# Four attention output chunks inside the first two FFN units, operand sums on VectorE, and LN2's mean from the residual add

## The chip, the cores and the metric

The kernel runs on one core of one Trainium2 chip. The metric is device time in microseconds (us) for one execution, the median over runs. The engines are named as in the profile: PE (TensorE, matrix products; PEld is its weight load), DVE (VectorE), ACT (ScalarE), POOL (GpSimd) and SP, which only issues DMA transfers here.

## What is computed

The input is one sequence of 2048 tokens with 1024 features, in bf16. Two blocks follow each other: linear attention with 32 heads, and a gated FFN with 3584 hidden features. A conditioning vector gives each block a shift, a scale and a gate.

```python
mod = silu(c) @ w_mod                    # six vectors: sa, ca, ga, sb, cb, gb
h = layernorm(x) * (1 + ca) + sa
q, k, v = heads(h @ wqkv)                # 32 heads of 32
pq, pk = phi(q), phi(k)                  # phi(t) = where(t > 0, t + 1, exp(t)) + 1e-6
o = (pq @ (pk^T v)) / (pq . sum(pk) + 1e-6)
x = x + ga * (o @ wo)
h = layernorm(x) * (1 + cb) + sb         # LN2
x = x + gb * ((gelu(h @ w_gate) * (h @ w_up)) @ w_down)
```

## The kernel before

**Units of work.** The 2048 tokens are 16 chunks of 128 (c0 to c15); four chunks are a group of 512 (sg 0 to 3). The attention output of a chunk is one `wo_chunk`: 16 matmuls (eight groups of heads by two halves of 512 columns) of the scaled queries `PQ[sg]` with the folded matrix `W2`, into two PSUM banks, `2*(c_%4)` and the next. Before that, DVE scales the queries by the reciprocal denominators (`pq_scale`, notes `pqs sg.half.g`; one half is the 256 tokens of two chunks); these come by DMA, spread over partitions (`rb_load`, 256 KB each). After it, DVE adds the result to the residual (`x1 c`, L1244 in the profile).

**LN2.** For chunks 0 to 7 `ln2(c_, True)` puts the work on ACT: a pass that sums the row (`sum`, L641), a pass that sums the squares about the mean (`sq`, L644), and the normalization (`xhat`, L633). Between them POOL turns the sums into mean and scale (L642 to L649). A DMA transpose (`T2 c`, L673) puts the chunk into `H2[0]` (chunks 0 to 3) or `H2[1]` (4 to 7), by way of four buffers `XL`. Then scale and shift are applied: `h2modb` on ACT for `H2[0]` (L723), `h2mod` on DVE for `H2[1]` (L694), two chunks at a time. Chunks 8 to 15 take their statistics on DVE, during the first pass's down projection.

**FFN.** It runs in two passes of 1024 tokens (p = 0, 1), each with 14 units of 256 hidden features (`unit`, L1429) and then the down projection (L1486). A unit is computed with seven products of half size instead of eight (a Strassen-like scheme): product k multiplies a sum of weight tiles (`TP`, made by `t_sum`, L1379) with a sum of operand parts. The operand sums `SS[0..3]` are made once per pass by `s_sums` (L1350), in fp32r: ss0 and ss2 on POOL in the first pass and ss2 on POOL in the second, the others on DVE; `ar_copy` makes one more operand on ACT. P1 and P2 need only `H2[0]` and the weights; P5 needs ss0, P6 ss1, P7 ss2, P3 ss3. The products collect in four pairs of banks, BA = 0, BE = 2, BB = 4, BC = 6, with copies on ACT (`pcp`, `escp`) and adds on DVE (`padd`, L1415) between them; then GELU on ACT (L1420) and the product with the up part on DVE (`yT`, L1424). `H2[1]` lies in the same memory as the buffers that `escp` and `gelu` write, so these must wait until the sums have read it.

**Down projection.** In each pass chunks 0 to 3 (`ga_`) collect in all eight banks, one quarter of the hidden features after another; then chunks 4 to 7 (`gb_`) use the same banks. `evac` takes a bank out: `x2a` multiplies by the gate (L1478), `x2b` adds to the residual (L1479), and a DMA writes the output. In the first pass the LN2 of chunks 8 to 15 and the sums for the second pass are queued on DVE before the evictions of chunks 0 to 3:

```python
s_sums(1, (2,))
for c_ in ga_:
    down_q(c_, (6, 4), last=True)
```

**What sets the order.** Every operation is recorded with the memory that it reads and writes; semaphore waits follow from that. Each engine executes its own list in order. PE's and SP's lists are in the order of the code. From the end of the key projections to the end of unit 1 of the first pass, `Sched.reorder` re-sorts the lists of DVE, ACT and POOL by a list schedule, with assumed costs and a due time for each operation. From unit 2 on, the code's order stands. SP has eight semaphore lanes: a transfer is issued only when the one eight places before it has landed.

Of the kernel before, what the change touches and what calls it, by code (L numbers as in the profile page):

```python
# [10 lines left out]
P = 128  # L11
# [302 lines left out]
def bass_adaLN_cond__linear_attn_block__geglu_ffn__prompt_kernel(  # L314
# [16 lines left out]
    with ExitStack() as es:  # L331
# [132 lines left out]

        def r_ss(i, k0=0, k1=NDC // 2):
            return [(OFF_SS[i] + k0 * 2048, OFF_SS[i] + k1 * 2048, f"ss{i}")]

# [33 lines left out]
        def r_rb(i, h, g0=0, g1=NG):  # L501
            return [(OFF_RB[i] + (h * NG + g0) * 1024, OFF_RB[i] + (h * NG + g1) * 1024, f"rb{i}")]

        def r_yt(fc, s0=0, s1=SP2):
            return [(OFF_YT + (fc * SP2 + s0) * 2, OFF_YT + (fc * SP2 + s1) * 2, "yT")]

# [128 lines left out]

        def ln_stats_act(c_, b_, rng, step):
            src = XALL[:, c_, :]
            sm, sq = STA[:, c_, 0:1], STA[:, c_, 1:2]
            rst, rmv = r_smc("st", c_, 48), r_smc("mv", c_, 8)
            if step == 0:  # L640
                sch.op(A, lambda e: e.activation(b_[:, :], src, ACTF.Identity, accum_out=sm), rd=r_x(c_), wr=rng + rst, note=f"sum {c_}")  # L641
                gop(lambda e: e.tensor_scalar(MVA[:, c_, 0:1], sm, -1.0 / D, None, op0=ALU.mult), rd=rst, wr=rmv, note=f"nmean {c_}")  # L642
            else:
                sch.op(A, lambda e: e.activation(b_[:, :], src, ACTF.Square, bias=MVA[:, c_, 0:1], accum_out=sq),  # L644
                       rd=r_x(c_) + rmv, wr=rng + rst, note=f"sq {c_}")
                gop(lambda e: e.tensor_scalar(VEA[:, c_:c_ + 1], sq, 1.0 / D, 1e-5, op0=ALU.mult, op1=ALU.add), rd=rst, wr=r_smc("ve", c_, 4), note=f"ve {c_}")
                gop(lambda e: e.tensor_tensor(RSA[:, c_:c_ + 1], VEA[:, c_:c_ + 1], NEGHALF[:, :], ALU.pow),
                    rd=r_smc("ve", c_, 4) + r_sm("neghalf"), wr=r_smc("rs", c_, 4), note=f"rstd {c_}")
                gop(lambda e: e.tensor_tensor(NMA[:, c_:c_ + 1], MVA[:, c_, 0:1], RSA[:, c_:c_ + 1], ALU.mult),  # L649
                    rd=rmv + r_smc("rs", c_, 4), wr=r_smc("nm", c_, 4), note=f"nm {c_}")  # L650
# [580 lines left out]
        def wo_mm(c_, b0, gs):  # L1231
# [9 lines left out]
            if gs[-1] == NG - 1:  # L1241
                for half in range(2):
                    pset_writer(b0 + half, last[half])
                sch.op(V, lambda e: e.tensor_tensor(XALL[:, c_, :], ps_all[:, b0 * 512:(b0 + 2) * 512], XALL[:, c_, :], ALU.add),  # L1244
                       prd=pr(b0) + pr(b0 + 1), rd=r_x(c_), wr=r_x(c_), note=f"x1 c{c_}")

# [53 lines left out]
        x_dma(NXR, 10)  # L1300
        rb_load(2)
        x_dma(10, 12)
        wo_mm(2, 4, E6[:4])
# [21 lines left out]
        def ln2(c_, on_act):  # L1325
            i = xl_i[0] % 4
            xl_i[0] += 1
            b_, rng = XL[i], r_2k(OFF_XL[i], f"xl{i}")
            if on_act:
                ln_stats_act(c_, b_, rng, 0)  # L1330
                ln_stats_act(c_, b_, rng, 1)
            else:
                ln_stats(c_, "B")
                ln_nm(c_)
            xhat_act(c_, b_, rng)
            h, ci = divmod(c_ % (2 * CPG), CPG)
            tdma(Q, H2[h][:, :, ci * P:(ci + 1) * P], b_[:, :], rng, r_h2(h, 0, NDC, ci * P, (ci + 1) * P), f"T2 {c_}")
# [9 lines left out]

        def s_sums(p, pool):
            def two(eng, i, k, in0, in1, op, rd):
                sch.op(eng, lambda e: e.tensor_tensor(SS[i][:, k:k + 2, :], in0, in1, op), rd=rd, wr=r_ss(i, k, k + 2), note=f"ssum{i} {p}.{k}")  # L1350
            a, b = H2
            for k in (0, 2):
                two(G if 0 in pool else V, 0, k, b[:, k:k + 2, :], b[:, ND2 + k:ND2 + k + 2, :], ALU.add, r_h2(1, k, k + 2) + r_h2(1, ND2 + k, ND2 + k + 2))
            for k in (0, 2):
                two(V, 1, k, S32[0][:, k:k + 2, :], a[:, k:k + 2, :], ALU.subtract, r_ss(0, k, k + 2) + r_h2(0, k, k + 2))
            for k in (0, 2):
                two(G if 2 in pool else V, 2, k, a[:, k:k + 2, :], b[:, k:k + 2, :], ALU.subtract, r_h2(0, k, k + 2) + r_h2(1, k, k + 2))
            for k in (0, 2):
                two(V, 3, k, a[:, ND2 + k:ND2 + k + 2, :], S32[1][:, k:k + 2, :], ALU.subtract, r_h2(0, ND2 + k, ND2 + k + 2) + r_ss(1, k, k + 2))

# [62 lines left out]
        def y_out(i, b, fc, h):  # L1423
            sch.op(V, lambda e: e.tensor_tensor(YT[:, fc, h * SGW:(h + 1) * SGW], GE[i][:, :], PS(b + 1), ALU.mult),  # L1424
                   rd=r_2k(OFF_GE[i], f"ge{i}"), prd=pr(b + 1), wr=r_yt(fc, h * SGW, (h + 1) * SGW), note="yT")

        held = [None]

        def unit(p, u):  # L1429
            more = u + 1 < NFP  # L1430
            f1, f2 = 2 * u, 2 * u + 1
            for t in range(2):
                prod(u, t, 1)
                if held[0]:
                    held[0]()
                    held[0] = None
                pcp(t)
            t_sum(u, 4)
            for t in range(2):
                prod(u, t, 5)  # L1440
                escp(t)
            if more:
                t_sum(u + 1, 0)
            for t in range(2):
                prod(u, t, 6)
                padd(t, BC)
            prod(u, 0, 2)
            ia = gi[0] % 2
            gelu(BA)
            prod(u, 1, 2)  # L1450
            if u + 2 < NFP:
                wt_dma(u + 2)
            y_out(ia, BA, f1, 0)
            if more:
                t_sum(u + 1, 1)
            for t in range(2):
                prod(u, t, 7)
                padd(t, BE)
            ie = gi[0] % 2
            gelu(BE)  # L1460
            y_out(ie, BE, f2, 1)
            prod(u, 0, 3)
            ic = gi[0] % 2
            gelu(BC)
            prod(u, 1, 3)
            y_out(ic, BC, f2, 0)
            if more:
                t_sum(u + 1, 3)
                t_sum(u + 1, 2)
            prod(u, 0, 4)  # L1470
            ib = gi[0] % 2
            gelu(BB)
            prod(u, 1, 4)
            held[0] = lambda: y_out(ib, BB, f1, 1)

# [7 lines left out]
        def down(c_, k, b, c0, c1, fcs, first, last):  # L1483
            ci, n, o = c_ % (2 * CPG), c1 - c0, None
            for fc in fcs:
                o = sch.op(T, lambda e, fc=fc: e.matmul(PS(b, 0, n), YT[:, fc, ci * P:(ci + 1) * P], WDT[fc // 4][:, fc % 4, c0:c1],  # L1486
                                                        start=first and fc == fcs[0], stop=last and fc == fcs[-1], skip_group_check=True),
                           rd=r_yt(fc, ci * P, (ci + 1) * P) + r_wd(fc), pwr=(pr(b) if first and fc == fcs[0] else ()), note=f"down c{c_} k{k} fc{fc}")
# [13 lines left out]
        ln2(0, True)  # L1502
        wt_dma(0)
        for c_ in range(3, NCH):
            if c_ == 3:
                pq_scale(1, 0, GH[0] + GH[1])
            if c_ == 4:
                pq_scale(1, 1, GH[0] + GH[1])
                rb_load(3, (0,))
            wo_chunk(c_, 2 * (c_ % 4))  # L1510
            if c_ in (5, 6, 7, 8):
                pq_scale(2, (c_ - 5) // 2, GH[(c_ - 5) % 2])
            if c_ == 5:
                sch.op(V, lambda e: e.tensor_scalar(CB1T[:, :], CBT[:, :], 1.0, None, op0=ALU.add), rd=r_sm("cbT"), wr=r_sm("cb1T"))
                rb_load(3, (1,))
            if c_ == 6:
                x_dma(12, 16)
            if c_ in (9, 10, 11):
                pq_scale(3, (c_ - 9) // 2, GH[(c_ - 9) % 2])
            if c_ == 11:  # L1520
                pq_scale(3, 1, GH[1])
            if 3 <= c_ < 10:
                ln2(c_ - 2, True)
            if c_ == 8:
                wt_dma(1)
            if c_ == 7:
                mod2_act(0)
            if c_ == 8:
                mod2(1, 0, 2)
            if c_ == 10:  # L1530
                mod2(1, 2, 2)
        s_sums(0, (0, 2))
        ar_copy(0)
        for k in range(4):
            t_sum(0, k)
        for p in range(2):
            c0 = p * 2 * CPG
            for u in range(NFP):
                unit(p, u)
                if p == 0 and u == 1:  # L1540
# [15 lines left out]
            if p == 0:  # L1556
                for c_ in range(2 * CPG, NCH):
                    ln2(c_, False)
                    if c_ == 3 * CPG - 1:
                        mod2_act(0)  # L1560
                    if c_ in (NCH - 3, NCH - 1):
                        mod2(1, c_ % CPG - 1, 2)
                s_sums(1, (2,))
            for c_ in ga_:
                down_q(c_, (6, 4), last=True)
            if p == 0:
                for c_ in gb_:
                    down_q(c_, (2, 3), first=True)
# [95 lines left out]
```

## Time and profile before

| | us |
|---|---|
| median of 3 runs (lowest to highest) | 821.17 (819.7 to 822.01) |
| the profiled execution | 821.04 |
| its span | 819.2 |
| PE busy | 794.4 (97%) |
| DVE busy | 571.1 (70%) |
| ACT busy | 311.2 (38%) |
| POOL busy | 55.1 (7%) |

The span runs from the first to the last instruction in the trace; the execution's time has 1.8 us more around it. PE is busy nearly throughout, so the time is the sum of PE's work at the granted clock and of its gaps. The profile's slices show in tenths how busy an engine is and which TensorE clock was granted (9 is 90% or more of full speed). A row of a timeline has start, length, engine, line, operation, out<-in and shape, and in brackets the idle time before it and what ended that.

### The profile page before, as it was taken

How to read it: one execution, taken by the hardware profiler on the slowest of the kernel's cores; microseconds unless marked ns; L12 is line 12 of the kernel's file. 1: busy time of each engine (PE TensorE's matmuls, PEld its weight loads, DVE VectorE, ACT ScalarE, POOL GpSimd, SP SyncE). 2: the span in 40 equal slices, each digit the busy share in tenths (PEclk: the TensorE clock that was granted, in tenths of full speed). 3: DMA queues.
4: the chain of work that ended last, by engine and by line, in shares of the span. 5: the costliest groups of instructions: out<-in, count | busy, mean ns of one | idle time of the engine just before them, and what ended most of it. 6: DMA issues, size and time to landing. Idle time of an engine off the chain costs nothing. (4 is left out here: it accounts for less than half of the span.)

```text
span 819.2 us, 10821 instructions
## 1 busy us (share of the span) xinstructions
PE 794.4 (97%) x3962; PEld 468.4 (57%) x4029; DVE 571.1 (70%) x990; ACT 311.2 (38%) x523; POOL 55.1 (7%) x108
## 2 busy tenths in 40 slices
PE   8999999999995999999999979999999999999998
PEld 4444446665443767767775434457767767744445
DVE  6799899973888788778776364278878788610522
ACT  2597642333594444444353400115444344400000
POOL 2121200000235000000001020000000000000000
PEclk9999999999997999999999998999999999999999
DMA  9789859569992334323228223222323323340100
GB/s 285 241 174 230 177 126 257 133 142 182 256 234 62 104 108 149 102 54 102 81 75 244 39 26 94 60 77 79 102 55 101 100 55 104 96 161 1 58 20 26
DMA packets 161324, 97.73 MB, mean 119 GB/s; under 512 B 68460, under 2 KB 148596, under 8 KB 160248
## 3 DMA queue, kind: packets, MB, share of 16 engines
q1 hardware_dynamic: 161256, 97.04, 46.2%
q8 instruction: 32, 0.52, 0.3%
q14 instruction: 20, 0.16, 0.1%
q10 hardware_dynamic: 16, 0.00, 0.0%
HBM read 78.92 MB, written 4.47 MB: 102 GB/s over the span
## 5 line engine op out<-in xcount | busy, mean ns | idle before, releaser
L1404 PE MATMUL ps_all<-ss,tp 128*128 128x512 f32 x896 | 227.5, 406 | 8.3 <-DVE h2b L694 5.5
L1486 PE MATMUL ps_all<-wd,yT 128*128 128x512 bf16 (+3 forms) x934 | 196.0, 370 | 6.9 <-DVE xall L1479 6.0
L1404 PEld LDWEIGHTS ps_all<-ss,tp 128*128 128x128 f32 x896 | 170.1, 190 | 50.5 <-DVE h2b L694 6.0
L1486 PEld LDWEIGHTS ps_all<-wd,yT 128*128 128x128 bf16 x952 | 90.7, 99 | 112.2 <-DVE xall L1479 6.5
L1420 ACT ACTIVATE ge<-ps_all 128x512 f32<-128x512 f32 x112 | 64.3, 596 | 137.6 <-DVE ps_all L1415 74.7
L1379 DVE TENSOR_TENSOR tp<-wt 128x512 fp32r<-128x512 bf16 x112 | 74.6, 689 | 44.8 <-PE ps_all L1486 25.3
L1404 PE MATMUL ps_all<-h2a,wt 128*128 128x512 bf16 x420 | 100.1, 380 | 1.9
L1424 DVE TENSOR_TENSOR yT<-ge,ps_all 128x512 bf16<-128x512 f32 x112 | 74.7, 685 | 33.3 <-PE ps_all L1404 30.6
L1415 DVE TENSOR_TENSOR ps_all<-ps_all,es 128x512 f32<-128x512 f32 x112 | 75.7, 697 | 20.3 <-PE ps_all L1404 20.3
L1478 DVE TENSOR_TENSOR ps_all<-ps_all,gbb 128x512 f32<-128x512 f32 (+3 forms) x34 | 22.6, 666 | 76.2 <-PE ps_all L1486 76.2
L1379 DVE TENSOR_TENSOR tp<-wt,tp 128x512 fp32r<-128x512 bf16 x112 | 72.2, 686 | 0.0
L1404 PEld LDWEIGHTS ps_all<-h2a,wt 128*128 128x128 bf16 x448 | 39.5, 98 | 54.2 <-issue 14.1
L903 PE MATMUL ps_all<-h1T,wq 128*128 128x512 bf16 x256 | 56.7, 379 | 0.0
L852 PE MATMUL ps_all<-wk,h1T 128*128 128x512 bf16 x239 | 55.3, 379 | 1.2 <-DMA wk<-in_A_wqkv_dram 0.5
L1236 PE MATMUL ps_all<-w,pq 128*128 128x512 bf16 x251 | 55.7, 379 | 0.3
L1404 PE MATMUL ps_all<-ar,tp 128*128 128x512 f32 x224 | 55.3, 389 | 0.0
L1409 ACT ACTIVATE ps_all<-ps_all 128x512 f32<-128x512 f32 x56 | 32.6, 582 | 52.6 <-PE ps_all L1404 50.9
L841 ACT ACTIVATE eb<-ps_all 128x512 f32<-128x512 f32 x64 | 36.4, 593 | 37.2 <-PE ps_all L852 15.1
L1404 PEld LDWEIGHTS ps_all<-ar,tp 128*128 128x128 f32 x224 | 42.0, 188 | 8.7
L1236 PEld LDWEIGHTS ps_all<-w,pq 128*128 128x128 bf16 x256 | 24.9, 98 | 30.1 <-ACT w L1170 0.4
L903 PEld LDWEIGHTS ps_all<-h1T,wq 128*128 128x128 bf16 x256 | 24.9, 98 | 30.0
L1412 ACT ACTIVATE es<-ps_all 128x512 f32<-128x512 f32 x56 | 33.5, 600 | 21.6 <-PE ps_all L1404 20.5
(117 smaller groups left out, 665.8 us busy)
## 6 DMA issues: line engine op xcount, KB each, us to landing
wt<-in_B_w_gate_dram SPq DMA_DIRECT2D x28, 512.0 KB, 4.1
wt<-in_B_w_up_dram SPq DMA_DIRECT2D x28, 512.0 KB, 4.9
wd<-in_B_w_down_dram SPq DMA_DIRECT2D x12, 1024.0 KB, 6.4
rb<-scr_rd SPq DMA_DIRECT2D x32, 256.0 KB, 5.7
wmst<-in_w_mod_dram SPq DMA_DIRECT2D x6, 1024.0 KB, 5.5
wmq<-in_w_mod_dram SPq DMA_DIRECT2D x8, 512.0 KB, 6.0
out_dram<-xall SPq DMA_DIRECT2D x31, 128.0 KB, 1.7
xall<-in_A_x_dram SPq DMA_DIRECT2D x3, 1024.0 KB, 9.5
```

The costliest lines, as they stand in the source:

```text
L841: sch.op(A, lambda e: e.activation(EB[i][:, :], PS(bank), ACTF.Exp), prd=pr(bank), wr=rng, note=f"{note}.exp")
L852: o = sch.op(T, lambda e, dc=dc: e.matmul(PS(bank), H1[sg][:, ci, dc, :], W_[:, dc, jg * 512:(jg + 1) * 512], start=(dc == 0), stop=(dc == ...
L903: o = sch.op(T, lambda e, dc=dc: e.matmul(PS(b), WQ[:, dc, qc * P:(qc + 1) * P], H1[sg][:, :, dc, :], start=(dc == 0), stop=(dc == NDC - 1 ...
L1236: last[half] = sch.op(T, lambda e, g=g, half=half: e.matmul(PS(b0 + half), PQ[sg][:, g, ci * P:(ci + 1) * P], W2[:, g, half * 512:(half + ...
L1379: sch.op(V, lambda e, t=t: e.tensor_tensor(TP[k][:, t, :, :], in0[:, t, :, :], in1[:, t, :, :], ALU.subtract), rd=r0[t:t + 1] + (r1[t:t + ...
L1404: o = sch.op(T, lambda e, l_=l_, r_=r_, dc=dc: e.matmul(PS(b), l_, r_, start=fresh and dc == 0, stop=dc == ND2 - 1, skip_group_check=True) ...
L1409: sch.op(A, lambda e: e.activation(PS(BB + t), PS(BA + t), ACTF.Copy), prd=pr(BA + t), pwr=pr(BB + t), note="pcp")
L1412: sch.op(A, lambda e: e.activation(ES[t][:, :], PS(BE + t), ACTF.Copy), prd=pr(BE + t), wr=r_2k(OFF_ES[t], f"es{t}"), note="escp")
L1415: sch.op(V, lambda e: e.tensor_tensor(PS(dst + t), PS(BB + t), ES[t][:, :], ALU.add), prd=pr(BB + t), rd=r_2k(OFF_ES[t], f"es{t}"), pwr=pr ...
L1420: sch.op(A, lambda e: e.activation(GE[i][:, :], PS(b), ACTF.Gelu_apprx_tanh), prd=pr(b), wr=r_2k(OFF_GE[i], f"ge{i}"), note="gelu")
L1424: sch.op(V, lambda e: e.tensor_tensor(YT[:, fc, h * SGW:(h + 1) * SGW], GE[i][:, :], PS(b + 1), ALU.mult), rd=r_2k(OFF_GE[i], f"ge{i}"), p ...
L1486: o = sch.op(T, lambda e, fc=fc: e.matmul(PS(b, 0, n), YT[:, fc, ci * P:(ci + 1) * P], WDT[fc // 4][:, fc % 4, c0:c1], start=first and fc ...
```

## The change

- **Order of the attention output and the FFN.** Before, `wo_chunk` 3 to 15 ran one after another, then unit 0. Now 3 to 11 run, then unit 0 with the products in the order 1, 2, chunk 12, 5, 6, 7, chunk 13, 3, chunk 14, 4, and unit 1 with chunk 15 between products 7 and 3. The late chunks use bank pairs BC and BA. All other units keep their order. `YT`, whose first rows share memory with `W2` and the second `RB` buffer, is filled in rotated order, so that units 0 to 5 stay out of it.
- **Transfers.** `rb_load(2)` is issued after the transpose of chunk 0 (first half) and of chunk 1 (second half), the residual rows of chunks 10 and 11 after the transpose of chunk 2, the weights of unit 0 after the transpose of chunk 4. `rb_load(3)`, the rows of chunks 12 to 15 (now in two transfers) and the weights of unit 1 are issued after the transpose of chunk 7.
- **Operand sums.** All are on DVE now. ss0, ss1 and ss2 are made in two halves of 256 tokens, ss3 in two halves of its columns as before.
- **Second pass.** The second `h2mod` group and all sums are recorded behind the evictions of chunks 0 to 3.
- **Mean of LN2.** For chunks 0 to 7 the residual add also writes the row sum, and ACT's `sum` pass is left out.

```diff
+                if c_ < 2 * CPG:
+                    sch.op(V, lambda e: e.scalar_tensor_tensor(XALL[:, c_, :], ps_all[:, b0 * 512:(b0 + 2) * 512], 1.0, XALL[:, c_, :],
+                                                               op0=ALU.mult, op1=ALU.add, accum_out=STA[:, c_, 0:1]),
...
-                ln_stats_act(c_, b_, rng, 0)
+                ln_stats_act(c_, b_, rng, 0, True)
...
+        def s_sum(p, i, j):
+            a, b = H2
+            k0, k1, s0, s1 = (2 * j, 2 * j + 2, 0, SGW) if i == 3 else (0, ND2, j * 2 * P, (j + 1) * 2 * P)
...
+            sch.op(V, lambda e: e.tensor_tensor(SS[i][:, k0:k1, s0:s1], in0, in1, op), rd=rd, wr=r_ss(i, k0, k1, s0, s1), note=f"ssum{i} {p}.{j}")
...
-        def unit(p, u):
+        def unit(p, u, order=(1, 5, 6, 2, 7, 3, 4)):
...
+            for k in order:
+                if isinstance(k, tuple):
+                    wo_chunk(*k)
+                    continue
...
         ln2(0, True)
-        wt_dma(0)
-        for c_ in range(3, NCH):
+        rb_load(2, (0,))
+        for c_ in range(3, 12):
...
+            if c_ == 3:
+                rb_load(2, (1,))
+            if c_ == 4:
+                x_dma(10, 12)
             if c_ == 6:
-                x_dma(12, 16)
...
+                wt_dma(0)
             if c_ == 7:
                 mod2_act(0)
             if c_ == 8:
                 mod2(1, 0, 2)
-            if c_ == 10:
-                mod2(1, 2, 2)
-        s_sums(0, (0, 2))
+                for i in range(3):
+                    s_sum(0, i, 0)
+        rb_load(3, (0,))
+        x_dma(12, 14)
+        rb_load(3, (1,))
+        x_dma(14, 16)
+        wt_dma(1)
+        mod2(1, 2, 2)
+        for i in range(3):
+            s_sum(0, i, 1)
+        for h in range(2):
+            s_sum(0, 3, h)
         ar_copy(0)
         for k in range(4):
             t_sum(0, k)
+        pq_scale(3, 0, GH[0] + GH[1])
+        pq_scale(3, 1, GH[0] + GH[1])
+        ORD = {0: (1, 2, (12, BC), 5, 6, 7, (13, BA), 3, (14, BA), 4), 1: (1, 5, 6, 2, 7, (15, BA), 3, 4)}
...
-                s_sums(1, (2,))
             for c_ in ga_:
                 down_q(c_, (6, 4), last=True)
             if p == 0:
+                mod2(1, 2, 2)
+                for i, j in ((0, 0), (0, 1), (1, 0), (1, 1), (2, 0), (2, 1), (3, 0), (3, 1)):
+                    s_sum(1, i, j)
```

## The prediction

> **What bounds the kernel now.** I read the page first. TensorE (PE) is busy for 794.4 of 819.2 us, so a change is worth what it takes out of PE's gaps and out of the stretches in which its clock is lowered. The slices show both: PE falls to 5 in the thirteenth slice and to 7 in the twenty-fourth, and the granted clock falls with it, or in the slice after.
>
> ```profile
> PE   8999999999995999999999979999999999999998
> PEclk9999999999997999999999998999999999999999
> ```
>
> The waits of PE say who ends these gaps (engine, line, releaser: us in total, times, longest):
>
> ```profile
> PE ps_all L1486 <- DVE xall L1479: 6.0, 1, 6.0
> PE ps_all L1404 <- DVE h2b L694: 5.5, 1, 5.5
> PE ps_all L1404 <- POOL ss L1350: 2.4, 1, 2.4
> PE ps_all L1404 <- DVE ss L1350: 0.4, 1, 0.4
> ```
>
> Three of them stand at one place, where the attention output ends and FFN unit 0 begins. PE's timeline there (start, us, line, operation):
>
> ```profile
> 248.97 1.89 PE L1404 MATMUL ps_all<-h2a,wt 128*128 128x512 bf16 x8
> 256.40 1.19 PE L1404 MATMUL ps_all<-ss,tp 128*128 128x512 f32 x2 [5.54 <-DVE h2b L694]
> 260.02 3.78 PE L1404 MATMUL ps_all<-ss,tp 128*128 128x512 f32 x8 [2.42 <-POOL ss L1350]
> 264.17 2.40 PE L1404 MATMUL ps_all<-ss,tp 128*128 128x512 f32 x6 [0.37 <-DVE ss L1350]
> 273.64 1.90 PE L1404 MATMUL ps_all<-h2a,wt 128*128 128x512 bf16 x8
> ```
>
> Product P1 starts in unit 0 at 248.97, in unit 1 at 273.64 and in unit 2 at 286.24. A steady unit thus takes 12.60 us and unit 0 took 24.67, 12.07 too many: 5.54 + 2.42 + 0.37 = 8.33 of waits, and 3.74 for the clock.
>
> The other place is the middle of the first pass's down projection. VectorE (DVE) works on the second pass's operands while PE waits for a PSUM bank:
>
> ```profile
> 477.97 5.79 DVE L694 TENSOR_SCALAR h2b<-h2b,cb1T,sbT 128x256 bf16<-128x256 bf16 x8 [5.86 <-DMA h2b<-xl]
> 483.67 2.35 DVE L1350 TENSOR_TENSOR ss<-h2b 128x1024 fp32r<-128x1024 bf16 x2
> 490.49 0.69 DVE L1478 TENSOR_TENSOR ps_all<-ps_all,gbb 128x512 f32<-128x512 f32 x1
> 491.21 0.69 DVE L1479 TENSOR_TENSOR xall<-ps_all,xall 128x512 bf16<-128x512 f32 x1
> ```
>
> The 224 matmuls of chunks 0 to 3 took 48.52 us (437.44 to 485.96); those of chunks 4 to 7 took 57.29 (485.96 to the next P1 at 543.25). The difference, 8.77, is 6.00 of wait and 2.77 of low clock. The windows of one us show the low clock:
>
> ```profile
> 491.00:492.00 1.00, 0.04 (x1) 0.55 0.00 0
> 497.00:498.00 1.00, 1.00 (x4) 0.54 0.20 68
> ```
>
> A mean of 0.55 is half clock for 0.9 of that us, so half clock ran from 491.1 to 497.9; the same reading gives 255.6 to 265.8 at the first place.
>
> **Second place: evictions first.** In the changed kernel DVE's queue has x2a and x2b of chunks 0 to 3 right behind LN statistics that end at 472.1, and the second h2mod group and all eight sums behind them. Chunk 0's first half has 160 + 8 matmuls before it: 437.44 + 168 x 0.2166 (48.52/224) = 473.8. A pair of evictions takes 1.41 us (490.49 to 491.90), a half of eight matmuls 1.73, so DVE keeps up; bank 0 is free at 475.3, PE asks for it at 486.0, and the last pair ends about 487.3. The 6.00 goes and with it the 2.77. What moves behind: h2mod, 2.1 without GpSimd beside it (row below), 8 sums at 1.17 (2.35 for two), 9.4, so they end about 499. They are wanted at the next P1, 534.5 by then: 35 us of cover. Next in DVE's queue, the tile sums wait for the down weights' buffers as before and end with the same distance to PE. Nothing else is late there. **-8.8 us.**
>
> **First place.** PE now does chunk 11, P1, P2, then chunk 12, then P5, P6, P7, chunk 13, P3, chunk 14, P4, and chunk 15 in unit 1. The work is the same, so only waits and clock count. Four chunks of 16 matmuls less at 0.216 put the end of chunk 11 at 248.97 - 13.8 = 235.1.
>
> What must be there for chunk 12 is pqs3 (the scaling of its operand), and DVE's queue, in the planner's order, puts this in front of it, behind x1 of chunk 11 (235.1 + 1.2 = 236.4): four tile sums at 0.605 (2.4), h2mod of chunks 4 and 5 (2.1), a tile sum (0.6), h2mod of chunks 6 and 7 (2.1), both halves of ssum0 (2.35), half of ssum1 (1.15) and the first pqs3 (0.6): 11.3, so chunk 12 starts at 247.7. The prices of h2mod are these, alone and beside GpSimd's sums, which are now gone:
>
> ```profile
> 244.87 2.13 DVE L694 TENSOR_SCALAR h2b<-h2b,cb1T,sbT 128x256 bf16<-128x256 bf16 x8
> 251.10 5.76 DVE L694 TENSOR_SCALAR h2b<-h2b,cb1T,sbT 128x256 bf16<-128x256 bf16 x8 [0.70 <-DMA h2b<-xl]
> ```
>
> Until 247.7 PE has P1 and P2 alone, 16 matmuls or 3.45: it idles 12.6 - 3.45 = 9.1 us, no less than the 8.33 before. The four chunks fill the time after the wait, not the wait.
>
> This holds if the last transpose (T2 of chunk 7) lands by 241.5. ScalarE (ACT) loses eight row sums (1.05 + 0.19 each, 9.9 us), but its order becomes one chain: square, GpSimd's three small steps, xhat, next chunk. The link, first to third step:
>
> ```profile
> 206.00 1.13 ACT L644 ACTIVATE xl<-xall,mv 128x1024 bf16<-128x1024 bf16 x1
> 209.73 1.24 ACT L633 ACTIVATE xl<-xall,nm,rs 128x1024 bf16<-128x1024 bf16 x1 [1.47 <-POOL nm L649]
> ```
>
> That is 4.97 to the end of xhat; the eight chunks range from 3.7 to 4.97, mean 4.17, and follow each other 0.1 closer. From 204.1, six links reach 228.6; then square 6, three h2modb (2.2), square 7, xhat 6, a h2modb and xhat 7 end at 236.4. A transpose landed 3.2 to 10.7 us after its issue (the 10.7 behind a full DMA queue). SP's new order has rb2 behind T2 0 and T2 1, the weights of unit 0 behind T2 4, and rb3, x12 to x15 and the weights of unit 1 all behind T2 7: some 3 MB less ahead of it, or 12 us at the 250 GB/s that the windows from 200 to 240 show. So I take 3.2 to 5: 239.6 to 241.4, just in time. rb3's first half is issued by 239.2 and lands about 6 us later (224 to 231.9 before), 245, ahead of its use at 247.1. rb2's halves land about 217 and 221, wanted at 219.3 and 226; x10 and wt have 3 us or more. POOL loses four sums of 2.1 to 3.1 us; the DVE sums that replace them are in the 11.3.
>
> The mean from the add: x1 becomes a scalar_tensor_tensor with a row sum, for which the trace has no row on DVE. From below, 0 (the 128x512 form from PSUM takes 686 ns, the plain add 692 to 697); from above the 0.19 of ACT's accumulator read; at the far end double time, 1.2 each. I take 0.1: chunks 0 to 2 are added 0.3 later and pqs1 still beats chunk 4 (207.1 against 207.6). Double time would stall chunk 4 by some 3 us. The Trainium skill, "VectorE: DVE Perf Modes", section "Two Vector instructions with no wait between them", counts an operation that writes its accumulator as two instructions; that speaks against the change, though only by an instruction of small size per chunk.
>
> After 247.7: P7's second half waits some 0.3 behind tsum2 and padd in DVE's queue, P6 of unit 1 0.3 for the second pcp, which ACT has behind both escp. Clock: waits of 5.5 and 6.0 both brought half clock, and this one is 6.4 after P2. Half clock then outlasted the wait by 5.9 us at the second place (2.8 lost) and by 3.74 of loss at the first; I take 2.4, since it could stay up (0) or cost 3.7. The skill's "TensorE: Matmul & The Clock Gate", Part 1, lets full clock return after one busy window of about 3.4 us; by that the loss would be an estimate of 1.7 and the sum 0.7 lower, but the 5.9 us row speaks against it. Sum: 9.1 + 0.6 + 2.4 = 12.1 against 12.07. **0.0 us.**
>
> **The sum.** The profiled execution took 821.04 around its span of 819.2, by the median of 821.17 within 0.13. 821.04 - 8.8 - 0.0 = **812.2**; I say 812.
>
> **Rivals.** (1) *The first place gains.* The clock stays up, or DVE's 11.3 is shorter: 2.4 to 4 us, 808 to 810. For: the clock fell only some 5 us after PE stopped. Against: 6.4 us of idleness. (2) *The last transpose is late.* Up to 241.5 it is hidden; each us later delays chunk 12 by one. At a link of 4.97 (0.8 more, seven times) it lands 4.6 past its cover: 817, and with a bank or rb2 wait 818.6. Against: the mean link. (3) *Slower.* The same landing with the slowest rows of both kinds: link 4.97 and 10.7 to land, T2 7 at 253, so 11.5 more, and 1.3 more of low clock: 825. It decides from a landing at 252 on. For: DMA was full from 195 to 250 and one transpose did take 10.7; against: 3 MB are moved out of its way. (4) *The second place keeps its wait*, as another release comes as late: 820 to 821; I find none.
>
> **Chances.** Forecast 0.50 (809.5 to 814.5), (1) 0.17, (2) 0.18, (4) and the bad end of (2) 0.07, (3) 0.08. A measurement of this kernel can tell 0.3%, 2.5 us, from no change: faster 0.85, same 0.07, slower 0.08. The range 807 to 818.5 leaves out some 2 in 10.
>
> **What would show it.** Right: no wait of L1486 on xall near 486 and full clock there; a PE wait of some 6 us before chunk 12, released by pqs; T2 7 landed before 242; P1 of unit 2 near 286. Wrong: chunks 12 to 15 without a wait ahead of them, an x1 row well over 1.4 us, a wait on h2b from a transpose, or gaps inside units 0 and 1.

## The result, and the profile after

The changed kernel takes 812.63 us (median of four runs, 812.12 to 813.46); the kernel before takes 821.17. The ratio is 0.9899, with a 95% interval of 0.9882 to 0.9916. The prediction said 812. The profiled execution took 812.12 us around a span of 810.2, against 821.04 and 819.2 before.

The page's slices first. The 7 in the twenty-fourth slice is gone; in the twelfth and thirteenth a 9 and a 5 have become an 8 and a 7, so the gap at the first place has moved and is still there.

```profile
PE   8999999999987999999999999999999999999998
PEclk9999999999998999999999999999999999999999
```

The waits of PE (engine, line, releaser: us in total, times, longest) agree: no wait of the down projection (now L1490) is left, and the three waits in unit 0 have become a long one in front of chunk 12 and two of 0.3 and 0.4 inside products.

```profile
PE ps_all L1241 <- DVE pq L1233: 8.0, 1, 8.0
...
PE ps_all L1412 <- ACT ps_all L1417: 0.4, 1, 0.4
PE ps_all L1412 <- ACT h2a L728: 0.3, 1, 0.3
```

PE's timeline at the second place, the first pass's down projection, is now one row:

```profile
437.08 96.87 PE L1490 MATMUL ps_all<-wd,yT 128*128 128x512 bf16 x448
533.79 1.89 PE L1412 MATMUL ps_all<-h2a,wt 128*128 128x512 bf16 x8
```

From its start to the next P1 it takes 96.71 us (533.79 - 437.08) where it took 105.81: 9.10 less. DVE's timeline shows why. The evictions run beside the matmuls, each pair waiting 0.30 for PE and not the other way round, and the operand work starts behind the last pair:

```profile
473.56 0.70 DVE L1482 TENSOR_TENSOR ps_all<-ps_all,gbb 128x512 f32<-128x512 f32 x1 [1.78 <-PE ps_all L1490]
474.29 0.69 DVE L1483 TENSOR_TENSOR xall<-ps_all,xall 128x512 bf16<-128x512 f32 x1
...
486.38 0.69 DVE L1483 TENSOR_TENSOR xall<-ps_all,xall 128x512 bf16<-128x512 f32 x1
486.98 2.13 DVE L699 TENSOR_SCALAR h2b<-h2b,cb1T,sbT 128x256 bf16<-128x256 bf16 x8
...
495.84 2.35 DVE L1367 TENSOR_TENSOR ss<-h2a,ss 128x1024 fp32r<-128x1024 bf16 x2
```

PE's timeline at the first place: P1, P2, chunk 12, the products P5 to P7, and further down the P1 of unit 2 at 285.88 (286.24 before).

```profile
235.20 2.81 PE L1412 MATMUL ps_all<-h2a,wt 128*128 128x512 bf16 x11
238.32 1.52 PE L1412 MATMUL ps_all<-h2a,wt 128*128 128x512 bf16 x5 [0.32 <-ACT h2a L728]
247.79 4.92 PE L1241 MATMUL ps_all<-w,pq 128*128 128x512 bf16 x16 [7.96 <-DVE pq L1233]
252.36 6.35 PE L1412 MATMUL ps_all<-ss,tp 128*128 128x512 f32 x24
...
274.17 1.17 PE L1412 MATMUL ps_all<-ss,tp 128*128 128x512 f32 x4 [0.36 <-ACT ps_all L1417]
...
285.88 1.90 PE L1412 MATMUL ps_all<-h2a,wt 128*128 128x512 bf16 x8
```

The windows of one us (PEclk is the column behind the five engines) show the half clock there. The means of 0.81 and 0.78 put it from 243.62 to 250.44:

```profile
243.00:244.00 1.00, 0.00 (x0) 0.00 (x0) 1.00 (x4) 0.75 (x1) 0.00 (x0) 0.81 1.35 459
250.00:251.00 1.00, 1.00 (x5) 0.40 (x4) 1.00 (x2) 0.00 (x0) 0.00 (x0) 0.78 1.19 309
```

Together: 0.36 less up to unit 2 and 9.10 less in the down projection make 9.46; pass 2 takes the same time in both (176.39 and 176.41 from its P1 to its down projection, which takes 97.01 in both), and 0.5 more passes behind the last matmul. That is the 9.0 by which the span is shorter.

### The profile page after: what moved, and what is told of

Its sections match the earlier page's. It is cut to its first block, busy times and chain, and to the rows that moved or that the text cites. A ratio compares the mean times of both kernels' runs of the same rounds, so it can differ in the third digit from the quotient of the medians.

```text
span 810.2 us, 10863 instructions
## 1 busy us (share of the span) xinstructions
PE 794.9 (98%) x4029; PEld 466.2 (58%) x4029; DVE 567.5 (70%) x1004; ACT 302.8 (37%) x507; POOL 38.5 (5%) x102
## 4 chain that ended last, share of the span: by engine, by line
PE 96%; DVE 1%; DMA 1%; issue 1%; ACT 0%; DVEq 0%; SPq 0%
PE ps_all L1412 43%; PE ps_all L1490 24%; PE ps_all L1241 7%; PE ps_all L908 7%; PE ps_all L857 6%; PE ps_all L872 6%; DMA mtb<-mb 1%; PE ps_all L923 1%; DVE h2b L699 0%; PE ps_all L890 0%; PE ps_all L1173 0%; PE ps_all L741 0%; DVE tp L1387 0%; DMA c<-in_c_dram 0%; PE ps_all L1200 0%
## 5 line engine op out<-in xcount | busy, mean ns | idle before, releaser
L1490 PE MATMUL ps_all<-wd,yT 128*128 128x512 bf16 (+3 forms) x952 | 193.9, 366 | 0.0
L1412 PEld LDWEIGHTS ps_all<-ss,tp 128*128 128x128 f32 x896 | 168.2, 188 | 41.5 <-DVE ps_all L1423 0.8
L1490 PEld LDWEIGHTS ps_all<-wd,yT 128*128 128x128 bf16 x952 | 90.0, 98 | 103.7 <-ACT ge L1428 0.5
L1412 PE MATMUL ps_all<-h2a,wt 128*128 128x512 bf16 x448 | 106.8, 380 | 0.5 <-ACT h2a L728 0.3
L1241 PE MATMUL ps_all<-w,pq 128*128 128x512 bf16 x256 | 57.9, 385 | 8.0 <-DVE pq L1233 8.0
L1417 ACT ACTIVATE ps_all<-ps_all 128x512 f32<-128x512 f32 x56 | 32.6, 582 | 48.8 <-PE ps_all L1412 48.6
```

What stands on the lines that cost most here:

```text
L1241: last[half] = sch.op(T, lambda e, g=g, half=half: e.matmul(PS(b0 + half), PQ[sg][:, g, ci * P:(ci + 1) * P], W2[:, g, half * 512:(half + ...
L1412: o = sch.op(T, lambda e, l_=l_, r_=r_, dc=dc: e.matmul(PS(b), l_, r_, start=fresh and dc == 0, stop=dc == ND2 - 1, skip_group_check=True) ...
L1490: o = sch.op(T, lambda e, fc=fc: e.matmul(PS(b, 0, n), YT[:, yrow(fc), ci * P:(ci + 1) * P], WDT[fc // 4][:, fc % 4, c0:c1], start=first a ...
```

## The experiments

Two questions were open. Is the second place the whole gain, and is it the order or the sums that left GpSimd? And why do four chunks moved into the wait at the first place bring nothing: which limit sets the restart there? For the second question each kernel is read by one distance, from P1 of unit 0 to P1 of unit 2: 50.68 us in the changed kernel. The kernel before is set beside it from the end of chunk 11, worked out as 235.14, to its P1 of unit 2: 51.10.

### e1_place2: only the order of the second place

```diff
 # on the kernel before
-                    if c_ in (NCH - 3, NCH - 1):
-                        mod2(1, c_ % CPG - 1, 2)
-                s_sums(1, (2,))
+                    if c_ == NCH - 3:
+                        mod2(1, 0, 2)
             for c_ in ga_:
                 down_q(c_, (6, 4), last=True)
             if p == 0:
+                mod2(1, 2, 2)
+                s_sums(1, (2,))
```

> The kernel before with the second place's edit alone: the second h2mod group and the sums stand behind the evictions of chunks 0 to 3 in DVE's queue; one of the four sums stays on GpSimd. Theory (DVE's queue holds the bank): the wait of 6.0 us and its low clock go, 9.0 less, about 812; h2mod still takes near 5.8 beside GpSimd, which nothing waits for. Rival (all sums must leave GpSimd, or another release comes as late): 818 to 821. If the first place had paid, this kernel would stay above the changed one by more than 1.

Measured: 812.34 us (810.97 to 812.82), ratio 0.9892 (0.9876 to 0.9909), no different from the changed kernel. The slow scaling beside GpSimd's sums is still there, as DVE's timeline shows, but it lies behind the evictions and nobody waits for it:

```profile
487.72 5.78 DVE L694 TENSOR_SCALAR h2b<-h2b,cb1T,sbT 128x256 bf16<-128x256 bf16 x8
```

So these few lines alone give the time of the whole change. The three waits of PE at the first place (4.8, 2.4 and 0.4; 5.5, 2.4 and 0.4 before) are still there.

### e2_place1: everything but that order

```diff
 # on the changed kernel
-                    if c_ == NCH - 3:
-                        mod2(1, 0, 2)
+                    if c_ in (NCH - 3, NCH - 1):
+                        mod2(1, c_ % CPG - 1, 2)
+                for i, j in (...): s_sum(1, i, j)
             for c_ in ga_:
                 down_q(c_, (6, 4), last=True)
             if p == 0:
-                mod2(1, 2, 2)
-                for i, j in (...): s_sum(1, i, j)
```

> The changed kernel with the second place in the old order (sums and second h2mod group ahead of the evictions, all sums on DVE). Theory: the first place alone is worth nothing, and the wait near 486 comes back, about 5 us since h2mod is 3.7 shorter and two more sums 2.3 longer, with some 3 of low clock: 820 to 821. Rival (the first place pays a part of the 8.5): 816 to 818.

Measured: 817.98 us (817.03 to 820.04), ratio 0.9967 (0.9953 to 0.9981). The expectation, a wait of about 5 us and some 3 of low clock, missed this: the wait is 3.31, the low clock costs 1.69 in PE's row, and the sums end at 487.4. DVE's and PE's timelines:

```profile
476.28 2.14 DVE L699 TENSOR_SCALAR h2b<-h2b,cb1T,sbT 128x256 bf16<-128x256 bf16 x8 [4.53 <-DMA h2b<-xl]
485.15 2.36 DVE L1367 TENSOR_TENSOR ss<-h2a,ss 128x1024 fp32r<-128x1024 bf16 x2
...
488.90 50.21 PE L1490 MATMUL ps_all<-wd,yT 128*128 128x512 bf16 x224 [3.31 <-DVE xall L1483]
```

What the expectation had counted came: from the start of the scaling to the first eviction DVE needs 11.14 us (476.28 to 487.42) where it needed 12.52, as the scaling takes 2.14 and not 5.79 with one pair of sums more. What it had not counted is that the scaling also started 1.31 earlier, 39.22 behind the start of the down projection and not 40.53: it waits there for the last transpose, which landed earlier; why was not traced. And half clock lasted 3.42 us, not 6.82.

The down projection takes 101.88 (437.06 to 538.94): 3.93 less than before, and 5.17 more than with the order changed. So not all of the 3.93 belongs to the sums: of the 2.69 that the wait is shorter, 1.38 are DVE's shorter work and 1.31 the transpose. The two edits overlap, as the order alone takes the whole 9.1 (e1). The first place, with 50.71 between the two P1, gains 0.4 at most.

### e3_pqs_first: chunk 12's operand ahead of the second scaling group

```diff
 # on the changed kernel, in DVE's list
+        move(DVE_, [(f"pqs3.0.{g}", 0) for g in (0, 2, 4, 6)], "h2mod 1.256.0")
```

> The changed kernel; in DVE's list the four pqs3 of chunk 12 stand ahead of the second h2mod group, ssum0 and half of ssum1. Both theories: chunk 12 starts near 243 instead of 247.8, when rb3 has landed, and the clock stays up. Theory (DVE's whole work sets the pace): the wait moves to P5 and P7, behind the sums; unit 2 starts 0.5 to 1.5 us earlier, 811. Rival (only the place of pqs3 in the queue counts): unit 2 starts 5 to 6 us earlier, 806 to 807. Second rival (rb3 is late): chunk 12 stays near 247.

Measured: 812.55 us. Chunk 12 starts 8.82 after P1 instead of 12.59, but PE then stops three times more, as its timeline shows:

```profile
244.63 5.65 PE L1241 MATMUL ps_all<-w,pq 128*128 128x512 bf16 x16 [4.17 <-DVE pq L1233]
250.75 2.12 PE L1412 MATMUL ps_all<-ss,tp 128*128 128x512 f32 x8 [0.48 <-DVE ss L1367]
253.02 2.12 PE L1412 MATMUL ps_all<-ss,tp 128*128 128x512 f32 x8 [0.16 <-DVE ss L1367]
257.03 2.38 PE L1412 MATMUL ps_all<-ss,tp 128*128 128x512 f32 x8 [1.89 <-DVE ps_all L1423]
```

The distance is 50.79. The clock did not stay up as both theories had it: half clock ran from 241.92 to 248.74, over most of chunk 12. An earlier chunk 12 alone is worth nothing: it runs slower, and P5, P6 and P7 need the sums that then come later.

### e4_filler and e4b_filler: matmuls in the wait

```diff
 # on the changed kernel
+                    if k[0] == 12:
+                        for _ in range(30):
+                            sch.op(T, lambda e: e.matmul(PS(BC), WT[0][:, 0, 0, 0:P], H2[0][:, 0, :], ...)
```

> The changed kernel with 30 matmuls of 128x512 ahead of chunk 12, into chunk 12's bank, which they fill with values that chunk 12 overwrites; they are extra work in PE's wait of 8 us. Theory (the clock falls with idleness): the clock stays full and the 1.3 us lost to it after 247.8 come back, 811; unit 2 starts 1.3 earlier. Rival (the clock does not matter here, or DVE sets the pace after chunk 12 anyway): no change, 812.

Measured: 827.24 us, and nothing about the clock. In the order of the code the buffer of unit 0's weights is by then assigned to the weights of unit 2, so that these matmuls wait for the next transfer into it, as PE's timeline shows:

```profile
257.49 8.13 PE L1445 MATMUL ps_all<-h2a,wt 128*128 128x512 bf16 x30 [16.09 <-DMA wt<-in_B_w_gate_dram]
```

The second form reads `H2[0]` for both operands.

> As the filler run before, but the 30 filler matmuls read only H2 parts that are ready; in the run before they read weights that the next transfer had yet to bring, and waited for that. Theory (the clock falls with idleness, and its loss is paid): full clock through chunk 12; P1 of unit 2 comes 49.4 us after P1 of unit 0 instead of 50.7, time about 811. Rival (DVE sets the pace after chunk 12, so a faster chunk 12 waits elsewhere): 50.2 to 50.7, no change.

Measured: 816.34 us. This one does not isolate the clock either: with more work in PE's list the planner drew up another list for DVE, with two halves of ss2 and tsum2 ahead of pqs3. Chunk 12 came at 251.14, and the clock had fallen anyway in the wait that was left:

```profile
251.14 6.48 PE L1241 MATMUL ps_all<-w,pq 128*128 128x512 bf16 x16 [3.23 <-DVE pq L1233]
```

In e5, w1, e4c, w2 and e7 the lists of DVE and ACT are therefore written out by hand for this part.

### e5_h2mod_act and e6_tsum_early: less in DVE's queue

```diff
 # e5, on the changed kernel: the second scaling group on ACT
-        mod2(1, 2, 2)
+        for dc in range(NDC):
+            sA, sB, rs_ = sc2(dc)
+            sch.op(A, lambda e, ...: e.activation(H2[1][:, dc, 256:512], H2[1][:, dc, 256:512], ACTF.Identity, bias=sB, scale=sA), ...)
 # e6, on the changed kernel: three tile sums ahead of the last add before the wait
+        move(DVE_, [("tsum0 u0", 0), ("tsum2 u0", 0), ("tsum1 u0", 0)], "x1 c11")
```

> The changed kernel; the second h2mod group of the first place (chunks 6 and 7, 2.1 us on DVE) is done by ACT, which idles there; DVE's list is otherwise the changed kernel's, with half of ssum1 one place earlier, and ACT's brcp of unit 0 stands behind its first gelu. Theory (DVE's whole work from chunk 11 on sets the pace): unit 2 comes 2.1 earlier, 48.6 after unit 0, 810. Rival (order or transfers set it): 50.2 to 50.7, 812.

> The changed kernel; three tile sums (1.8 us) stand ahead of chunk 11's add in DVE's list, where DVE waits 2.2 us for PE. Theory (DVE's whole work): unit 2 comes 1.8 earlier, 48.9 after unit 0, 810.3, if the weights have landed by 233. Rival: no change, 50.2 to 50.7.

Measured: 811.99 and 812.00 us, distances 49.48 and 50.23. Both restart PE about as much earlier as expected (chunk 12 is 10.67 and 10.79 behind P1, not 12.59), and both give part of it back. PE's timeline of e6, and its windows:

```profile
246.52 6.30 PE L1241 MATMUL ps_all<-w,pq 128*128 128x512 bf16 x16 [6.15 <-DVE pq L1233]
252.47 6.33 PE L1412 MATMUL ps_all<-ss,tp 128*128 128x512 f32 x24
```

```profile
241.00:242.00 1.00, 0.00 (x0) 0.00 (x0) 1.00 (x5) 0.02 (x1) 0.00 (x0) 0.86 1.14 238
251.00:252.00 1.00, 1.00 (x3) 0.30 (x2) 0.00 (x0) 0.00 (x0) 0.00 (x0) 0.52 1.25 302
```

Half clock from 241.72 to 251.96: the whole of chunk 12 ran at it and took 5.95 to P5, where the changed kernel took 4.57.

### w1: both, and pqs3 earlier

```diff
 # DVE's list around the wait
-x1 c11, tsum0, tsum2, tsum1, h2mod(4,5), tsum1, h2mod(6,7), ssum0, ssum0, ssum1, pqs3 x4, ssum1, ssum2, x1 c12
+tsum0, tsum2, tsum1, x1 c11, tsum0, h2mod(4,5), ssum0, ssum1, tsum1, pqs3 x4, ssum0, ssum1, x1 c12, ssum2
 # and the second scaling group on ACT, as in e5
```

> The changed kernel with both: three tile sums ahead of chunk 11's add, the second h2mod group on ACT; and pqs3 of chunk 12 ahead of the second half of ssum0. Theory (DVE's whole work): 3.9 less, unit 2 46.8 after unit 0, and up to 1.3 more if the clock stays up: 807 to 808.5. Rival (the parts hide behind each other): 810 to 812.

Measured: 811.05 us (809.26 to 811.66), ratio 0.9870 (0.9853 to 0.9886), distance 49.59: 1.1 less, not 3.9. PE's timeline, then DVE's:

```profile
245.09 6.46 PE L1241 MATMUL ps_all<-w,pq 128*128 128x512 bf16 x16 [4.17 <-DVE pq L1233]
251.19 4.03 PE L1412 MATMUL ps_all<-ss,tp 128*128 128x512 f32 x16
256.29 2.41 PE L1412 MATMUL ps_all<-ss,tp 128*128 128x512 f32 x8 [1.07 <-DVE ss L1367]
```

```profile
251.65 1.23 DVE L1254 TENSOR_TENSOR xall<-ps_all,xall 128x1024 bf16<-128x1024 f32 x1 [2.42 <-PE ps_all L1241]
```

The slow chunk 12 holds up DVE for 2.42 us, and ss2 and P7 come later with it.

### e4c_filler and w2: the clock kept up

```diff
 # e4c: on the changed kernel, both lists kept as they were; w2: on w1, with 18 matmuls
+                    if k[0] == 12:
+                        for _ in range(36):
+                            sch.op(T, lambda e: e.matmul(PS(BC), H2[0][:, 0, 0:P], H2[0][:, 0, :], ...)
```

> The changed kernel with the instruction lists of VectorE and ScalarE kept exactly as they were, and 36 matmuls of 128x512 (operands: ScalarE's finished half of the FFN input alone) between P2 of unit 0 and chunk 12, whose results nobody reads: at 0.2166 each they fill 7.8 of the 7.96 us of wait. Theory (the wait costs half clock behind it): chunk 12 still starts at 247.8, no window near it is under 0.95, it takes 3.45 in place of 4.57, P1 of unit 2 comes 49.4 us after P1 of unit 0 (50.68 in the changed kernel), and the time is 1.3 lower, 810.8. Rival (VectorE's queue sets the pace behind chunk 12 as well): the clock stays up, but P5 or P7 waits for the sums, and at most 0.5 is gained: 50.2, 811.7.

> The kernel of w1 with 18 matmuls of 128x512 between P2 of unit 0 and chunk 12, whose results nobody reads (3.9 of the 4.17 us of wait there). Theory (in w1 the low clock in chunk 12 took back what the shorter queue of VectorE gave: chunk 12 took 6.10 in place of 3.45, and VectorE stood idle for 2.42 because of it): chunk 12 starts at 245.1 and takes 3.45, P1 of unit 2 comes 47.2 us after P1 of unit 0 (49.59 in w1), and the time is 2.4 below w1, 808.7. Rival (VectorE's queue is the bound after all): P7 and the chunks behind wait longer and the time stays at 810.5 to 811.

Measured: e4c 810.21 us (one run) and w2 808.60 us (five runs, 808.25 to 809.04); w2's ratio to before is 0.9851 (0.9833 to 0.9868), clear of the changed kernel's interval. Both profiles have a mean clock of 1.000. PE's timeline of e4c:

```profile
239.70 7.93 PE L1445 MATMUL ps_all<-h2a 128*128 128x512 bf16 x36
247.83 3.63 PE L1241 MATMUL ps_all<-w,pq 128*128 128x512 bf16 x16 [0.19 <-DVE pq L1233]
251.10 6.34 PE L1412 MATMUL ps_all<-ss,tp 128*128 128x512 f32 x24
```

and of w2:

```profile
245.51 3.63 PE L1241 MATMUL ps_all<-w,pq 128*128 128x512 bf16 x16 [0.26 <-DVE pq L1233]
248.79 3.99 PE L1412 MATMUL ps_all<-ss,tp 128*128 128x512 f32 x16
253.84 2.42 PE L1412 MATMUL ps_all<-ss,tp 128*128 128x512 f32 x8 [1.06 <-DVE ss L1367]
```

Chunk 12 takes 3.27 and 3.28 to P5. The distances are 49.40 (expected 49.4) and 46.74 (expected 47.2). P7 waits as long in w2 (1.06) as in w1 (1.07), so that wait is not the clock's: in both, ss2 is made behind chunk 12's add.

### e7_act_sum: the row sums back on ACT

```diff
 # on the changed kernel; ACT's list: sum 0, sq 0, sum 1, xhat 0, sq 1, sum 2, xhat 1, ...
-                if c_ < 2 * CPG:
+                if c_ < 0:
...
-                ln_stats_act(c_, b_, rng, 0, True)
+                ln_stats_act(c_, b_, rng, 0)
```

> The changed kernel with LN2's row sums of chunks 0 to 7 back on ScalarE (the add on VectorE is the plain one again), each placed where ScalarE waits for GpSimd's small steps of the chunk before; VectorE's list is kept. Theory (the chain square, GpSimd, xhat has a gap of 1.3 to 2.05 us in every link and a sum with its read takes 1.24): the links stay near 3.85, the last transpose is issued by 235.5, chunk 12 starts at 247.8 +- 0.3, and the time is 812.1 +- 0.5, so that the mean from the add is worth nothing here. Rival (eight sums lengthen the chain by 9.9 us): the last transpose is issued at 244.7 and lands at 248, 6.4 past its cover of 241.6, chunk 12 starts at 254, and the time is 818.5.

Measured: 814.91 us, between the two, in one run. 1.5 us of it lie ahead of the edit: the adds of chunks 0 to 2, the first changed instructions, already start at 204.10 instead of 202.59, and w2, without this edit, has the same P1 (236.72). In the place itself the distance is 51.65, 0.97 more. PE's timeline:

```profile
239.45 1.25 PE L1412 MATMUL ps_all<-h2a,wt 128*128 128x512 bf16 x5 [1.94 <-ACT h2a L728]
242.60 1.12 PE L1412 MATMUL ps_all<-h2a,wt 128*128 128x512 bf16 x3 [1.89 <-ACT ps_all L1417]
...
250.10 5.11 PE L1241 MATMUL ps_all<-w,pq 128*128 128x512 bf16 x16 [4.54 <-DVE pq L1233]
```

The last normalization comes 4.4 us later, counted from the same start (239.41 against 233.53, less 1.5): the sums fit between the links only partly. Most of this is covered, as DVE's queue would have held chunk 12 until 12.59 behind P1 in any case; it starts 13.39 behind it. So the mean from the add is worth about 1 us here. That rests on one run and on the positions in it.

### All of them by one sum

Three terms account for each change of the distance to within 0.3 us: when chunk 12 starts behind P1, how long it takes to P5, and how long P5 to P7 wait behind it. The times of changed, w1 and w2 are medians, the others one run each.

| kernel | chunk 12 starts | half clock | to P5 | later waits | distance | change by the terms | change measured | time |
|---|---|---|---|---|---|---|---|---|
| changed | 12.59 | 6.82 | 4.57 | 0 | 50.68 | | | 812.63 |
| e3 | 8.82 | 6.82 | 6.12 | 2.05 | 50.79 | -0.17 | +0.11 | 812.55 |
| e5 | 10.67 | 6.82 | 5.29 | 0 | 49.48 | -1.20 | -1.20 | 811.99 |
| e6 | 10.79 | 10.24 | 5.95 | 0 | 50.23 | -0.42 | -0.45 | 812.00 |
| w1 | 8.81 | 6.84 | 6.10 | 1.07 | 49.59 | -1.18 | -1.09 | 811.05 |
| e4c | 12.61 | none | 3.27 | 0 | 49.40 | -1.28 | -1.28 | 810.21 |
| w2 | 8.79 | none | 3.28 | 1.06 | 46.74 | -4.03 | -3.94 | 808.60 |
| e7 | 13.39 | 3.40 | 4.76 | 0 | 51.65 | +0.99 | +0.97 | 814.91 |

## Why the prediction was right

**Second place, -8.8: measured -9.10.** Each step came as worked out: first eviction 473.56 (473.8), last one ended 487.07 (487.3), sums ended 498.19 (499), next P1 533.79 (534.5), no wait near 486 and full clock. e1 shows that the order is the cause and the whole gain. What the prediction did not separate, e2 does: taking the sums off GpSimd shortens DVE's work ahead of the evictions by 1.38 as long as the old order stands, and is worth nothing once it is changed.

**First place, 0.0: measured -0.36 to unit 2.** The step that decides it held to 0.1: DVE's queue of 11.3 us put chunk 12 at 247.7 by the prediction and at 247.79 by the trace, 12.59 behind P1, of which 3.47 are work and 9.1 idle. (The prediction set this 9.1 beside waits of 8.33 before. The two are not counted alike: by the records of waits it is 0.32 + 7.96 = 8.28 now.) Around it three small terms were off and nearly cancel, so that it is luck how near the sum came: 12.1 predicted, 11.7 measured.

- *The clock*, predicted 2.4, cost 1.30 (4.57 against 3.27 for chunk 12); e4c shows it, as it alone takes 1.28 away. The mis-sized term came from carrying over a tail of 5.9 us behind a wait, and a loss of 3.74 that was not all the clock's: PE worked for 6.62 us of the half clock before, which makes a loss of 3.31 by estimate, at half speed. The tail is no constant. Half clock lasted 6.82 us again, but PE idled through the first 4.17 of them, so that only 2.65 fell on work. The half clock that the prediction read before (491.1 to 497.9, and 255.6 to 265.8) lasts 6.8 and 10.2, which are two and three times 3.4. The rule that the prediction set aside is the one that the runs support: the Trainium skill, "TensorE: Matmul & The Clock Gate", Part 1, describes a free-running window of about 3.4 us and full clock after a busy one. The row of 5.9 us did not speak against it: in the first of those two windows PE worked for 2.55 us only, in the second throughout.
- *Small waits*, predicted 0.6, were 0.36 (L1417 in unit 1); the 0.3 of P7 behind tsum2 did not come.
- *A term that was missing*: 0.9 us. Four chunks of 3.45 and two units of 12.60 make 39.0; with 9.1, 0.36 and 1.30 that is 49.8, and the distance is 50.68. e4c has it too (39.0 + 9.1 + 0.36 + 0.9 = 49.4). In e4c's rows, from start to start and against a steady unit, it is 0.97 in the products that stand next to chunks (P5 to P7, P3 and P4 in unit 0, P7 and P3 in unit 1), 0.37 in P1 and P2 of unit 0 (3.47 counted, 3.10 in a steady unit) and 0.26 by which the wait of 0.36 costs more than its length; the four chunks take 0.70 less (13.10, not 13.8).

**The last transpose** was issued at 234.83 (236.4 predicted), because the links of ACT's chain followed each other by 3.84 on average and not 4.07 (4.17 less 0.1), and `h2mod` used it at 241.60 without a wait. With the 3.1 us to landing that the view of DMA issues gives for it, it was there about 237.9 (predicted 239.6 to 241.4); rival (2) needed it 3.6 us later, (3) some 14. P2 was done earlier too, at 239.84, so that the wait in front of chunk 12 is 7.96 and not some 6; chunk 12's start does not hang on that. e7 shows how near (2) was: with ACT slower by 4.4 us, `h2mod` waits 0.71 for the transpose and chunk 12 slips by 0.8.

**The mean from the add** cost 0.0 where 0.1 was taken. DVE's timeline shows two instructions for each add; from the first of three adds to the operation behind them it is 3.44 (202.59 to 206.03) where it was 3.41:

```profile
202.59 1.22 DVE L1250 SCALAR_TENSOR_TENSOR xall<-ps_all,xall 128x1024 bf16<-128x1024 f32 x1 [4.08 <-PE ps_all L1241]
203.74 0.08 DVE L1250 DVE_READ_ACCUMULATOR xall<-ps_all,xall 128x1 f32 x1
203.74 1.22 DVE L1250 SCALAR_TENSOR_TENSOR xall<-ps_all,xall 128x1024 bf16<-128x1024 f32 x1
```

That an operation with an accumulator output is two instructions is what the Trainium skill says in "VectorE: DVE Perf Modes", section "Two Vector instructions with no wait between them"; the second one, 0.08 long, is hidden.

**Rival (1)**, a first place that gains by a clock that stays up or a shorter queue, put 808 to 810 on the two. Neither came by itself in this change. Made on purpose, they give 810.2 (the clock, e4c, one run), 811.0 (the queue, w1, whose interval overlaps that of the changed kernel) and 808.6 (both, w2). **Rival (4)** had no release behind it, and none was seen.

## What to carry to other kernels

Read for each wait of the busiest engine what its releaser did just before it, and whether that work had a deadline: here it had 35 us to spare and stood in front of evictions that had none, so exchanging the two gave the whole gain, and the other edits beside it gave nothing that a run can tell. Work moved into an engine's wait gains nothing while another engine's queue sets the end of that wait; shorten that queue first, and count the time at half clock behind every wait as part of its price. When a gap of a few microseconds can't be closed, matmuls whose results nobody reads can hold the clock up through it, and may be worth more than an earlier restart.

## What was not expected of the hardware

**Half clock came in whole multiples of 3.41 us, on a grid that runs on through the kernel.** The lengths worked out from the windows' means are 3.40 (e7), 3.42 (e2's second place), 6.82 (before's second place, e2's first, changed kernel, e3, e5), 6.84 (w1, e4b), 10.24 (before's first place, e1, e6) and 17.06 (e4). Two kernels have two such stretches. In the kernel before they begin at 255.58 and 491.10, and 235.52 is 69 times 3.413; in e2 they begin at 243.68 and 489.44, and 245.76 is 72 times 3.413. Before's window at the first place (the one at the second stands in the prediction), and e2's at the second:

```profile
255.00:256.00 1.00, 0.00 (x0) 0.00 (x0) 1.00 (x1) 0.12 (x1) 1.00 (x1) 0.79 0.00 0
489.00:490.00 1.00, 1.00 (x4) 0.35 (x4) 0.97 (x2) 0.00 (x0) 0.00 (x0) 0.72 0.20 71
```

On that grid half clock ended behind a window of 3.41 us in which PE was busy for 2.65 or more in the changed kernel, e2 and e3 to e7; with 2.55 (before, second place), 2.35 (w1) or 2.03 (e6) it went on for another. Busy time alone does not settle it: in e1 a window with 2.68 did not end it. So e6, which restarted PE 1.8 us earlier in its place (10.79 against 12.59 behind P1), stayed at half clock for a whole window more than the changed kernel, as its restart left 2.03 us of work in the second window.

**The clock fell between 1.35 and 5.14 us after PE had stopped** (e6: from 240.37 to 241.72; before, second place: from 485.96 to 491.10). It fell behind a window in which PE had been busy for 1.66 us (e6), and stayed up behind one with 1.63 (before, second place) and one with 1.52 (e7), so what makes it fall is open. In e2 it fell 0.5 us after PE had started again, at 489.44, and the down projection then lost 1.69 us (50.21 against 48.52 for 224 matmuls) behind a wait of only 3.31.
